# Regrouping tokens by batch and moving transposes to the DMA crossbar in a windowed-attention plus MLP kernel

## The chip, the cores and the metric

The kernel runs on one core of a Trainium2 chip. The metric is the device time of one execution in microseconds (us); smaller is better. Times quoted are medians of all runs of a kernel. Runs marked slow (a lower granted TensorE clock, or over 1.5% above the kernel's fastest run) are left out of ratios. Engine names in the profile: PE is TensorE (PEld is its weight load), DVE is VectorE, ACT is ScalarE, POOL is GpSimd, and SP is SyncE, which here only issues DMAs. A q behind an engine's name means its queue: SPq lines are DMAs that SyncE issues.

## The reference

Eight batches of 576 tokens, eight heads of 64 channels. Causal attention looks back over 64 tokens only; its output `x` (4608 x 512) goes through a layer norm and a two-layer MLP with a residual:

```python
mask   = (rel >= 0) & (rel < 64)                      # sliding window, causal
attn   = softmax(where(mask, q @ k.T / 8, -1e9)) @ v
x      = attn.transpose(0, 2, 1, 3).reshape(8, 576, 512)
xn     = (x - mean(x)) / sqrt(var(x) + 1e-6) * g_ln
out    = x + relu(xn @ w_ch1) @ w_ch2                 # 512 -> 2048 -> 512
```

## The kernel before

The MLP works on groups of four 128-token blocks, 512 tokens at a time, nine groups in all. A group is 32 units of PE work: 16 of layer 1 (four 128x512 matmuls each), then 16 of layer 2. Between the units the kernel slots in the attention of the next batch: score steps (`s_mm`, one or two windows of 64 tokens), the mask on VectorE (`s_mask`), and B steps (`b_step`), which multiply the weights of two windows by V, normalise, take row statistics and leave a centred fp16 block `z`. `zt_step` transposes `z` into the group's `zT`, the moving operand of layer 1. `1/sqrt(var)` of a group (`rstd`, computed partly on GpSimd) scales the output only at the end.

A batch is 4.5 blocks, so in this kernel the groups of four straddle the batches. `vB` is V moved by 64 partitions, made by two copies from SBUF to SBUF (325 and 260 KB) on the GpSimd DMA queue. The parts, with cuts:

```python
def make_vB(b, lo, hi):
    nc.gpsimd.dma_start(out=vB[b][64:128, lo:hi], in_=vA[b][0:64, lo:hi])
    l0, l1 = max(lo - 1, 0), min(hi - 1, 4)
    nc.gpsimd.dma_start(out=vB[b][0:64, l0 + 1:l1 + 1], in_=vA[b][64:128, l0:l1])

def w1_cast(i):
    ...
    nc.gpsimd.tensor_copy(out=w1g[...], in_=t)

def zt_step(kblk, eng=None):
    ...
    ztp = ps_t.tile([128, NKC, 128], FP16, tag="tp", name=f"ztp_{kblk}")
    for kc in range(NKC):
        nc.tensor.transpose(out=ztp[:, kc, :], in_=z[:, 128 * kc:128 * (kc + 1)], identity=ident16)
    ...                                   # copied to zT by ScalarE

# groups 1 to 6: the slots of batch b = g + 1, in units of the group's 32
ss = [2, 7, 12, 17, 22]                   # score steps
sb = [x + 3 for x in ss]                  # B steps, three units after the scores they use
at(13, group_stats, g)
at(0, make_vB, b, 0, 5)
for kblk in range((NW * b) // 2, (NW * (b + 1)) // 2):
    si = sb[((2 * kblk + 1) - NW * b + 1) // 2]
    at(si, b_step, kblk)
    at(max(si + 4, 17 if kblk // 4 > b else 0), zt_step, kblk, "act")
```

The softmax here doesn't subtract the row's maximum and nothing guards it: scores larger than these inputs give would overflow.

## Time and profile before

The first three runs gave 354.6 us (352.95 to 357.05). The lines below are from the page of the profiled execution: the span; busy time, share and instruction count of each engine; then PE's busy share and the granted TensorE clock in 40 equal slices, in tenths; last, the chain of waits that ended last, as shares of the span.

```profile
span 351.7 us, 6792 instructions
...
PE 323.0 (92%) x2778; PEld 159.5 (45%) x2778; DVE 169.0 (48%) x300; ACT 172.9 (49%) x301; POOL 120.5 (34%) x214
...
PE   2662998889999999999999999999999999999995
...
PEclk9999999999999999999999999999999999999998
...
PE 82%; DVE 7%; DMA 4%; SPq 3%; ACT 3%; issue 0%; POOL 0%
```

PE is busy 92% of the span, the clock is full almost everywhere, and 82% of the chain is PE itself. Only the first nine slices (about 80 us) show real holes. The windows view says the same by stage. Its columns are the stretch, its length, then busy time and instruction count of PE, PEld, DVE, ACT and POOL, then the mean granted clock, the DMA share and GB/s. The first stretch is group 1, the second is groups 2 to 5:

```profile
core 0: us, PE busy (x) PEld busy (x) DVE busy (x) ACT busy (x) POOL busy (x), PEclk, DMA share, GB/s
80.30:116.80 36.50, 36.24 (x358) 18.09 (x357) 20.51 (x39) 22.49 (x40) 14.35 (x26) 1.00 0.67 174
116.80:258.60 141.80, 141.74 (x1324) 70.42 (x1322) 75.52 (x139) 84.35 (x146) 50.62 (x88) 1.00 0.60 148
```

Groups 2 to 5 take 141.80 us and PE is busy for 141.74 of them. Whatever takes PE work out of this stretch should shorten the kernel by as much.

| where (timeline and windows of before) | us |
|---|---|
| first layer-1 matmul of group 0 | 35.5 |
| first layer-1 matmul of group 1 | 80.3 |
| first layer-1 matmul of group 2 | 116.8 |
| groups 2, 3, 4, 5 | 35.7, 35.2, 35.7, 35.2 |
| group 6 to the end of the span | 93.1 |

### The profile page before, as it was taken

Reading aid. Unit: us, or ns where it says so; the run is one execution under the profiler, and the core shown is the slowest. Engines: PE = TensorE matmul, PEld = TensorE weight load, DVE = VectorE, ACT = ScalarE, POOL = GpSimd, SP = SyncE. Lnnn points to the kernel's source line nnn. Section 1 sums busy time; section 2 is a strip of 40 time slices with the busy share of each in tenths; the row PEclk is TensorE's granted clock in tenths of the full one; section 3 lists DMA queues with packets and bytes.
Section 4 is the critical chain, followed back from the end, with each engine's and each line's share of the span. In section 5 each row is a group of like instructions: output and inputs, shape, how many; then the busy total and the mean of one; then the engine's idle time right before and its main releaser. Section 6 shows DMA issues by size and latency. Waiting matters only on the chain.

```text
span 351.7 us, 6792 instructions
## 1 busy us (share of the span) xinstructions
PE 323.0 (92%) x2778; PEld 159.5 (45%) x2778; DVE 169.0 (48%) x300; ACT 172.9 (49%) x301; POOL 120.5 (34%) x214
## 2 busy tenths in 40 slices
PE   2662998889999999999999999999999999999995
PEld 1331353454445444544454445444544444444442
DVE  1488066965576167714771667136716671012011
ACT  2331455138735774477447744774477515603600
POOL 4566664863094009400940085008500202001000
PEclk9999999999999999999999999999999999999998
DMA  7999999879934591359235923492310011011011
GB/s 246 248 300 329 177 295 277 264 149 275 254 96 124 172 247 51 100 181 259 55 102 183 234 65 112 150 273 59 114 61 2 2 60 62 0 62 60 0 47 72
DMA packets 73743, 51.16 MB, mean 145 GB/s; under 512 B 47568, under 2 KB 63952, under 8 KB 73712
## 3 DMA queue, kind: packets, MB, share of 16 engines
q1 hardware_dynamic: 72528, 46.41, 49.3%
q0 software_dynamic: 1184, 4.33, 5.3%
q8 instruction: 21, 0.34, 0.4%
q14 instruction: 10, 0.08, 0.1%
HBM read 36.96 MB, written 9.44 MB: 132 GB/s over the span
## 4 chain that ended last, share of the span: by engine, by line
PE 82%; DVE 7%; DMA 4%; SPq 3%; ACT 3%; issue 0%; POOL 0%
DMA w1s_124<-in_moe_w_ch_dram 2%; SPq L115 2%; DMA w1s_442<-in_moe_w_ch_dram 1%; PE ch_1_4109 L328 1%; PE ch_1_3592 L328 1%; PE ch_1_2526 L328 1%; PE ch_1_3076 L328 1%; PE ch_1_2010 L328 1%; PE ch_0_1954 L328 1%; PE ch_0_1406 L328 1%; PE ch_0_3535 L328 1%; PE ch_0_3019 L328 1%; PE ch_0_2470 L328 1%; PE ch_1_1462 L328 1%; PE ch_2_3667 L328 1%; PE ch_2_4177 L328 1%
## 5 line engine op out<-in xcount | busy, mean ns | idle before, releaser
L315 PEld LDWEIGHTS <-w1g 128*128 128x128 f16 x576 | 53.2, 98 | 61.4 <-issue 5.7
L328 PEld LDWEIGHTS <-hrT_4446 128*128 128x128 f16 x64 | 6.3, 98 | 7.5
L328 PEld LDWEIGHTS <-hrT_4255 128*128 128x128 f16 x64 | 6.2, 98 | 7.6
L303 POOL TENSOR_TENSOR rstmp_4532<-rstdg_4531 128x4 f32<-128x4 f32 x2 | 0.4, 198 | 25.4 <-DVE rstdg_4531 L298 25.3
L353 PEld LDWEIGHTS <-hrT_526 128*128 128x128 f16 x64 | 5.8, 98 | 6.7 <-issue 0.8
L338 DVE SCALAR_TENSOR_TENSOR osb_4383<-ch_0_4366,rstdg_4340,xn_3504 128x512 f32<-128x512 f32 x1 | 0.8, 751 | 16.6 <-PE ch_0_4366 L328 16.6
L338 DVE SCALAR_TENSOR_TENSOR osb_4574<-ch_0_4557,rstdg_4531,xn_3935 128x512 f32<-128x512 f32 x1 | 0.8, 751 | 16.2 <-PE ch_0_4557 L328 16.2
L328 PEld LDWEIGHTS <-hrT_3796 128*128 128x128 f16 x64 | 5.8, 98 | 5.8
L328 PEld LDWEIGHTS <-hrT_2216 128*128 128x128 f16 x64 | 5.7, 98 | 5.4
L328 PEld LDWEIGHTS <-hrT_1668 128*128 128x128 f16 x64 | 5.6, 98 | 5.4
L303 POOL TENSOR_TENSOR rstmp_2956<-rstdg_2955 128x4 f32<-128x4 f32 x2 | 0.4, 198 | 22.5 <-DVE rstdg_2955 L298 22.4
L328 PEld LDWEIGHTS <-hrT_2732 128*128 128x128 f16 x64 | 5.6, 98 | 5.4
L303 POOL TENSOR_TENSOR rstmp_4002<-rstdg_4001 128x4 f32<-128x4 f32 x2 | 0.4, 198 | 22.5 <-DVE rstdg_4001 L298 22.4
L303 POOL TENSOR_TENSOR rstmp_1892<-rstdg_1891 128x4 f32<-128x4 f32 x2 | 0.4, 198 | 22.5 <-DVE rstdg_1891 L298 22.4
L328 PEld LDWEIGHTS <-hrT_3280 128*128 128x128 f16 x64 | 5.6, 98 | 5.4
L328 PEld LDWEIGHTS <-hrT_1096 128*128 128x128 f16 x64 | 5.6, 98 | 5.4
L303 POOL TENSOR_TENSOR rstmp_3472<-rstdg_3471 128x4 f32<-128x4 f32 x2 | 0.4, 197 | 21.9 <-DVE rstdg_3471 L298 21.9
L303 POOL TENSOR_TENSOR rstmp_2408<-rstdg_2407 128x4 f32<-128x4 f32 x2 | 0.4, 198 | 21.9 <-DVE rstdg_2407 L298 21.8
L319 ACT ACTIVATE hrT_4446<-hps_0_4447 128x512 f16<-128x512 f32 x1 | 0.6, 597 | 14.1 <-PE hps_0_4447 L315 14.1
L181 DVE COPY qkT_1_493<-tp_0_0_600 128x1024 f16<-128x1024 f16 x1 | 1.2, 1225 | 11.6 <-PE tp_0_0_600 L188 11.6
L188 PE MATMUL tp_0_0_146<-ident_99,qk_0_0_0_142 128*128 128x128 f16 x8 | 1.0, 311 | 5.8 <-POOL qk_0_0_0_142 L96 5.8
L303 POOL TENSOR_TENSOR rstmp_4341<-rstdg_4340 128x4 f32<-128x4 f32 x2 | 0.4, 198 | 17.3 <-DVE rstdg_4340 L298 17.2
(1320 smaller groups left out, 951.2 us busy)
## 6 DMA issues: line engine op xcount, KB each, us to landing
v_0_114<-in_v_dram SPq DMA_DIRECT2D x4, 256.0 KB, 7.5
v_1_478<-in_v_dram SPq DMA_DIRECT2D x4, 256.0 KB, 6.4
v_2_581<-in_v_dram SPq DMA_DIRECT2D x4, 256.0 KB, 4.7
v_3_1297<-in_v_dram SPq DMA_DIRECT2D x4, 256.0 KB, 5.9
v_4_1845<-in_v_dram SPq DMA_DIRECT2D x4, 256.0 KB, 7.3
v_5_2361<-in_v_dram SPq DMA_DIRECT2D x4, 256.0 KB, 6.0
v_6_2909<-in_v_dram SPq DMA_DIRECT2D x4, 256.0 KB, 6.4
v_7_3425<-in_v_dram SPq DMA_DIRECT2D x4, 256.0 KB, 6.7
```

The source lines that it names most:

```text
L115: nc.sync.dma_start(out=v32[b][:, c], in_=v[b, :, 128 * c:128 * c + 128, :].rearrange("h s d -> s h d"),)
L181: nc.vector.tensor_copy(out=out, in_=in_)
L188: nc.tensor.transpose(out=tp[:, i, j, :], in_=src[:, i, j], identity=ident16)
L303: nc.gpsimd.tensor_tensor(out=ab, in0=rs, in1=rs, op=ALU.mult)
L315: nc.tensor.matmul(out=hps, lhsT=w1g[:, kc, 128 * hc:128 * (hc + 1)], rhs=zT[g][:, kc, :], start=(kc == 0), stop=(kc == NKC - 1),)
L319: nc.scalar.activation(out=hrT[:, hc, :], in_=hps, func=AF.Relu, bias=0.0, scale=1.0)
L328: nc.tensor.matmul(out=ch[kb], lhsT=hrT[:, hc, 128 * kb:128 * (kb + 1)], rhs=w2s[:, hc, :], start=(hc == 0), stop=(hc == NHC - 1),)
L338: nc.vector.scalar_tensor_tensor(out=o, in0=ch[kb], scalar=rstd[g][:, kb:kb + 1], in1=x_norm[kblk][:, :, :].rearrange("p h d -> p (h d)"), ...
L353: nc.tensor.matmul(out=ch[kb], lhsT=hrT[:, hc, 128 * kb:128 * (kb + 1)], rhs=w2s[:, hc, :], start=(hc == 0), stop=(hc == NHC - 1),)
```

## The change

Four things at once. (1) A group is now the first 512 tokens of one batch; the eight rests of 64 tokens form group 8. (2) From group 2 on, `z` is transposed by the DMA crossbar, issued on the SP queue, instead of PE and ScalarE. (3) At the start, the W1 casts move from GpSimd to ScalarE and interleave with the B steps of batch 0, most VectorE copies for `vB` of batch 0 (five of eight) become DMAs, the loads of W2 and of batch 1's V move ahead of those of the rests, and the q/k transposes of later work move from group 0 to group 1. (4) Three of four B steps in a group follow a score step directly ("bunched"), to save PE's switching between kinds of matmul. Pools shrink to make room (`xn` 13 to 8 buffers plus 4 for the rests, block pool 4 to 3). The core of the diff, with cuts:

```diff
@@ w1_cast
-        nc.gpsimd.tensor_copy(
+        nc.scalar.copy(
...
@@ zt_step
+        if g >= 2:
+            nc.sync.dma_start_transpose(out=zT[g][:, :, 128 * kb:128 * kb + 128], in_=z)
+            return
...
@@ b_step
-        halves = [divmod(2 * kblk + r, NW) for r in range(2)]
+        halves = [(2 * kb + r, NW - 1) if sfx else (g, 2 * kb + r) for r in range(2)]
...
@@ start
+    make_vB(0, 2, 4)
...
+    for i in range(4):
+        b_step(0, i)
+        if i >= 1:
+            zt_step(0, i - 1)
+        if i < 3:
+            s_mm(0, sets0[i + 2], True)
         w1_cast(i)
         w1_load(i + 4)
+    zt_step(0, 3)
...
@@ group 0
-            at(17, group_stats, 0)
+            at(18, group_stats, 0)
...
@@ groups 1 to 6
-            ss = [2, 7, 12, 17, 22]
-            sb = [x + 3 for x in ss]
+            ss = [1, 6, 11, 16, 21] if g > 1 else [6, 10, 14, 17, 21]
+            for kb in range(4):
+                at(([11, 16, 21, 25] if g > 1 else [14, 17, 21, 25])[kb], b_step, b, kb)
+                at([16, 21, 25, 29][kb], zt_step, b, kb)
+            if b % 2 == 1:
+                at(28, b_step, NGRP - 1, b // 2)
+                at(32, zt_step, NGRP - 1, b // 2)
```

The last block of a group now has its B step at unit 25 and its transpose at unit 29 of 32, just before the group that needs it.

More of the change, by code (lines that the diff above doesn't have):

```diff
@@ L43 @@
     scale = 1.0 / (D ** 0.5)
-    out_f = out.flatten_outer_dims()
     p_const = ctx.enter_context(tc.tile_pool(name="pconst", bufs=1))
@@ L52 @@
     p_pt = ctx.enter_context(tc.tile_pool(name="ppt", bufs=6))
-    p_xn = ctx.enter_context(tc.tile_pool(name="pxn", bufs=13))
-    p_blk = ctx.enter_context(tc.tile_pool(name="pblk", bufs=4))
+    p_xn = ctx.enter_context(tc.tile_pool(name="pxn", bufs=8))
+    p_blk = ctx.enter_context(tc.tile_pool(name="pblk", bufs=3))
     p_grp = ctx.enter_context(tc.tile_pool(name="pgrp", bufs=2))
@@ L136, in make_vB0 @@
         nc.vector.tensor_copy(out=vB[0][64:128, c, :, 0:D], in_=v32[0][0:64, c])
-        nc.vector.tensor_copy(out=vB[0][0:64, c + 1, :, 0:D], in_=v32[0][64:128, c])
+        if c == 0:
+            nc.vector.tensor_copy(out=vB[0][0:64, 1, :, 0:D], in_=v32[0][64:128, 0])
     def make_vB(b, lo, hi):
@@ L239, in v_rhs, with b_step @@
         return vB[b][:, w // 2, h, :]
-    def b_step(kblk):
-        g, kb = divmod(kblk, 4)
-        xn = p_xn.tile([128, H, D], FP32, tag="xn", name=f"xn_{kblk}")
-        x_norm[kblk] = xn
+    def b_step(g, kb):
+        kblk = f"{g}_{kb}"
+        sfx, nb = ("r", 4) if g == NGRP - 1 else ("", None)
+        xn = p_xn.tile([128, H, D], FP32, tag="xn" + sfx, name=f"xn_{kblk}", bufs=nb)
+        x_norm[(g, kb)] = xn
         xps = ps_x.tile([128, H, 128], FP32, tag="xps", name=f"xps_{kblk}")
-        halves = [divmod(2 * kblk + r, NW) for r in range(2)]
+        halves = [(2 * kb + r, NW - 1) if sfx else (g, 2 * kb + r) for r in range(2)]
         for h in range(H):
@@ L263, in b_step @@
         if g not in mvg:
-            mvg[g] = p_grp.tile([128, 4, 2], FP32, tag="mvg", name=f"mvg_{g}", bufs=3)
+            mvg[g] = p_grp.tile([128, 4, 2], FP32, tag="mvg" + sfx, name=f"mvg_{g}", bufs=1 if sfx else 2)
         nc.vector.bn_aggr(out=mvg[g][:, kb, :], in_=stats)
         z = p_blk.tile([128, DM], FP16, tag="z", name=f"z_{kblk}")
-        zsd[kblk] = z
+        zsd[(g, kb)] = z
         nc.vector.scalar_tensor_tensor(
@@ L271, in b_step, with zt_step @@
         )
-    def zt_step(kblk, eng=None):
-        g, kb = divmod(kblk, 4)
-        z = zsd.pop(kblk)
+    def zt_step(g, kb, eng="act"):
+        z = zsd.pop((g, kb))
         if g not in zT:
-            zT[g] = p_grp.tile([128, NKC, 512], FP16, tag="zT", name=f"zT_{g}")
-        ztp = ps_t.tile([128, NKC, 128], FP16, tag="tp", name=f"ztp_{kblk}")
+            sfx = "r" if g == NGRP - 1 else ""
+            zT[g] = p_grp.tile([128, NKC, 512], FP16, tag="zT" + sfx, name=f"zT_{g}", bufs=1 if sfx else 2)
+        if g >= 2:
+            nc.sync.dma_start_transpose(out=zT[g][:, :, 128 * kb:128 * kb + 128], in_=z)
+            return
+        ztp = ps_t.tile([128, NKC, 128], FP16, tag="tp", name=f"ztp_{g}_{kb}")
         for kc in range(NKC):
@@ L323, in l2 @@
         def l2(kb, part):
-            kblk = 4 * g + kb
             if part == 0:
@@ L335, in add_out @@
         def add_out(kb):
-                kblk = 4 * g + kb
-                o = p_blk.tile([128, DM], FP32, tag="osb", name=f"osb_{kblk}")
-                nc.vector.scalar_tensor_tensor(
-                    out=o, in0=ch[kb], scalar=rstd[g][:, kb:kb + 1],
-                    in1=x_norm[kblk][:, :, :].rearrange("p h d -> p (h d)"), op0=ALU.mult, op1=ALU.add,
-                )
-                nc.sync.dma_start(out=out_f[128 * kblk:128 * (kblk + 1), :], in_=o)
-        for hc in range(NHC):
-            units.append(lambda hc=hc: l1(hc))
+            o = p_blk.tile([128, DM], FP32, tag="osb", name=f"osb_{g}_{kb}")
+            nc.vector.scalar_tensor_tensor(
+                out=o, in0=ch[kb], scalar=rstd[g][:, kb:kb + 1],
+                in1=x_norm[(g, kb)][:, :, :].rearrange("p h d -> p (h d)"), op0=ALU.mult, op1=ALU.add,
+            )
+            if g == NGRP - 1:
+                for r in range(2):
+                    nc.sync.dma_start(out=out[2 * kb + r, 512:S, :], in_=o[64 * r:64 * r + 64])
+            else:
+                nc.sync.dma_start(out=out[g, 128 * kb:128 * kb + 128, :], in_=o)
         def l2_hc(i):
@@ L359, in l2_hc @@
                     add_out(kb)
+        for hc in range(NHC):
+            units.append(lambda hc=hc: l1(hc))
         if hc_outer:
@@ L401 @@
         cast_v(0, c, c + 1)
+    make_vB(0, 2, 4)
     sets0 = [[0], [1, 2], [3, 4], [5, 6], [7]]
     s_mm(0, sets0[0], True)
-    make_vB0(0)
     s_mm(0, sets0[1], True)
-    make_vB0(1)
-    for i in range(2, 5):
-        s_mm(0, sets0[i], True)
-        b_step(i - 2)
-        if i < 4:
-            make_vB0(i)
-        if i >= 3:
-            zt_step(i - 3, "act")
-    b_step(3)
-    zt_step(2, "act")
-    zt_step(3, "act")
-    for i in range(4):
+    for c in range(2):
+        make_vB0(c)
+    for i in range(4):
+        b_step(0, i)
[3 more added lines that the diff above has]
+            s_mm(0, sets0[i + 2], True)
         w1_cast(i)
         w1_load(i + 4)
+    zt_step(0, 3)
     load_qk(1, 0)
     load_qk(1, 1)
-    load_qk_rem(0)
-    load_v_rem(0)
+    load_v(1, 0, 4)
     for i in range(4):
         w1_cast(i + 4)
+        w2_load(i)
     cast_qk(1, 0)
     cast_qk(1, 1)
-    cast_qk_rem(0)
-    cast_v_rem(0)
-    load_v(1, 0, 4)
-    load_qk_rem(1)
-    load_v_rem(1)
     alloc_v(1)
@@ L437 @@
     alloc_qkT(1)
-    make_vB(0, 4, 5)
-    cast_v(1, 0, 4)
-    cast_v_rem(1)
-    make_vB(1, 0, 5)
-    for i in range(8):
-        w2_load(i)
-        w2_cast(i)
+    cast_v(1, 0, 4)
+    make_vB(1, 0, 4)
+    for i in range(8):
+        w2_cast(i)
+        if i < 4:
+            w2_load(i + 4)
+    load_qk_rem(0)
+    load_v_rem(0)
+    cast_qk_rem(0)
+    cast_v_rem(0)
+    make_vB(0, 4, 5)
+    load_qk_rem(1)
+    load_v_rem(1)
     SETS = [[0], [1, 2], [3, 4], [5, 6], [7, 8]]
@@ L456 @@
         if g == 0:
-            at(8, t_main, 1, 0, 0, 1)
-            at(9, t_main, 1, 1, 0, 1)
-            at(10, t_main, 1, 0, 1, 1)
-            at(11, t_main, 1, 1, 1, 1)
-            at(12, t_rem, 0)
-            at(12, cast_qk_rem, 1)
-            for i, j in enumerate((12, 13, 14, 15)):
-                at(j, s_mm, 1, SETS[i])
-                at(j, s_mask, 1, SETS[i])
-                if i == 0:
-                    at(14, s_mm, 0, [8])
-                    at(14, s_mask, 0, [8])
-            at(20, t_rem, 1)
@@ L470 @@
-            sb = [17, 18, 19, 20, 21]
-            at(17, group_stats, 0)
-        else:
-            ss = [2, 7, 12, 17, 22]
-            sb = [x + 3 for x in ss]
+            at(9, t_main, 1, 0, 0, 1)
+            at(10, t_main, 1, 1, 0, 1)
+            at(11, t_main, 1, 0, 1, 1)
+            at(12, t_main, 1, 1, 1, 1)
+            for i, j in enumerate((12, 13, 14, 15, 15)):
+                at(j, s_mm, 1, sets0[i])
+                at(j, s_mask, 1, sets0[i])
+            for kb in range(4):
+                at(17 + kb, b_step, 1, kb)
+                at(19 + kb, zt_step, 1, kb)
@@ L475 @@
+            at(18, group_stats, 0)
+            e = 13
+        else:
             at(13, group_stats, g)
-        if g == 1:
-            at(0, s_mm, 1, SETS[4])
-            at(0, s_mask, 1, SETS[4])
-            at(3, b_step, 8)
-            at(7, zt_step, 8, "act")
-        if b < B:
-            if g > 0:
-                for i, ws in enumerate(SETS):
-                    at(ss[i], s_mm, b, ws)
-                    at(ss[i] + 1, s_mask, b, ws)
-                at(0, alloc_vB, b)
-                at(0, make_vB, b, 0, 5)
-            for kblk in range((NW * b) // 2, (NW * (b + 1)) // 2):
-                if kblk == 8 and g == 0:
-                    continue
-                si = sb[((2 * kblk + 1) - NW * b + 1) // 2]
-                at(si, b_step, kblk)
-                dz = 2 if g == 0 else 4
-                at(max(si + dz, 17 if kblk // 4 > b else 0), zt_step, kblk, "act")
+            e = 16
@@ new lines @@
+        if 0 < g and b < B:
+            if g == 1:
+                at(0, t_rem, 0, 0)
+                at(0, cast_qk_rem, 1)
+                at(0, cast_v_rem, 1)
+                at(0, make_vB, 1, 4, 5)
+                at(0, s_mm, 0, [8])
+                at(0, s_mask, 0, [8])
+                at(1, alloc_qkT, 2)
+                at(1, t_main, 2, 0, 0, 0)
+                at(1, t_main, 2, 1, 0, 1)
+                at(2, t_rem, 1, 0)
+                at(2, load_qk_rem, 2)
+                at(2, load_v_rem, 2)
+                at(3, t_main, 2, 0, 1, 0)
+                at(3, t_main, 2, 1, 1, 1)
+                at(4, s_mm, 1, [8])
+                at(4, s_mask, 1, [8])
+                at(7, cast_qk_rem, 2)
+                at(7, cast_v_rem, 2)
+                at(8, b_step, NGRP - 1, 0)
+                at(12, zt_step, NGRP - 1, 0)
+                at(12, t_rem, 2, 0)
+                va = 8
+            else:
+                va = 0
+            at(va, alloc_vB, b)
+            at(va, make_vB, b, 0, 5)
+            ss = [1, 6, 11, 16, 21] if g > 1 else [6, 10, 14, 17, 21]
+            for i, ws in enumerate(SETS):
+                at(ss[i], s_mm, b, ws)
+                at(ss[i] + 1, s_mask, b, ws)
+            for kb in range(4):
+                at(([11, 16, 21, 25] if g > 1 else [14, 17, 21, 25])[kb], b_step, b, kb)
[3 more added lines that the diff above has]
+                at(32, zt_step, NGRP - 1, b // 2)
@@ L495 @@
         if b + 1 < B:
             n = b + 1
-            e = 16 if g > 0 else 12
             at(e - 12, load_qk, n, 0)
             at(e - 11, load_qk, n, 1)
-            at(e - 10, load_qk_rem, n)
+            if g > 0:
+                at(e - 10, load_qk_rem, n)
             at(e - 6, load_v, n, 0, 4)
-            at(e - 6, load_v_rem, n)
+            if g > 0:
+                at(e - 6, load_v_rem, n)
             at(e - 1, cast_qk, n, 0)
             at(e + 1, cast_qk, n, 1)
-            at(e + 3, cast_qk_rem, n)
+            if g > 0:
+                at(e + 3, cast_qk_rem, n)
@@ L506 @@
             at(e + 5, alloc_v, n)
             at(e + 5, cast_v, n, 0, 4)
-            at(e + 6, cast_v_rem, n)
-            at(e + 5, alloc_qkT, n)
-            at(e + 8, t_main, n, 0, 0, 0)
-            at(e + 10, t_main, n, 1, 0, 0)
-            at(e + 12, t_main, n, 0, 1, 0)
-            at(e + 13, t_main, n, 1, 1, 0)
-            at(e + 15, t_rem, n, 0)
+            if g > 0:
+                at(e + 6, cast_v_rem, n)
+            if g > 0:
+                at(e + 5, alloc_qkT, n)
+                at(e + 8, t_main, n, 0, 0, 0)
+                at(e + 8, t_main, n, 1, 0, 0)
+                at(e + 12, t_main, n, 0, 1, 0)
+                at(e + 12, t_main, n, 1, 1, 0)
@@ L515 @@
+            if g > 0:
+                at(e + 16, t_rem, n, 0)
         for i, u in enumerate(units):
```

## The prediction

> **What bounds the kernel now.** TensorE. The page shows PE busy 323.0 of 351.7 us (92%), and the chain of waits lies 82% on PE. The stage windows show two regimes. From 80.3 us (first layer-1 matmul of group 1) to about 348 us PE is busy almost without a wait: groups 1 to 6 take 36.5, 35.7, 35.2, 35.7, 35.2, 33.5 us, groups 7 and 8 (no attention left) 27.7 us each, which is 128 matmuls at 0.216 us. Before 80.3 us PE is idle some 25 us: the first MLP matmul starts at 35.5 us, after VectorE's chain for batch 0 (vB copies 0.4 to 1.15 us each), and the DMA share is about 1.0 until 65 us (17 MB of inputs).
>
> **Costs, from the trace.**
> 1. Transposes: 28 of 36 row blocks leave PE. In the timeline the four transposes of a block cost 0.22 us start to start: 28 x 0.22 = 6.2 us, all in PE-bound groups. ScalarE loses 28 x 0.59 us, off the chain.
> 2. Bunching: a lone score step costs 0.44 us and a lone B step 0.47 us between layer matmuls, of which about 0.2 us is switching. Three of four B steps per group now follow a score step directly: estimate 0.4 us per group, 2.5 us in all.
> 3. New wait: layer 1 of a group waits for the crossbar DMA of z block 3, which the SP queue issues behind the output store of block 2. PE has six layer-2 units (0.87 us each), two q/k transposes and a remainder left, about 6.6 us. VectorE needs 2.8 us for z and 0.75 us for that output, SP 0.4 us, so the DMA has about 2.5 us. The 256 KB stores land in 2.0 us, the SBUF copies in 3.8 to 4.4 us; I estimate 2 to 4 us for 128 KB transposed: 0 to 1.5 us at each of six boundaries, estimate 3 us. The Trainium skill ("VectorE: DVE Perf Modes", The three transpose paths) gives 1309 ns for a crossbar 128x128 against 390 ns on TensorE; no run here shows the former yet.
> 4. Start: five VectorE copies fall away and W1 casts leave GpSimd, so zT of group 0 should be ready near 32 us instead of 35. But W1 loads 4 to 7 wait for ScalarE casts, and ReLU 0 stands behind casts 4 to 7 (about 1 us each), so the third layer-1 unit starts near 37 us (before 38.9). Group 0's outputs still wait for rstd on GpSimd behind the batch-2 casts, which are DMA-bound. Batch 2's q/k transposes (2 us of PE) move from group 0, where PE had slack, into group 1. Group 1 starts at 76 to 82 us and lasts about 38: net gain 2 us, quite uncertain.
>
> **Sum.** 354.6 - 6.2 - 2.5 + 3 - 2 = 347; as the start could gain more, 346 us, 339 to 353. Faster by over 2%: 0.52; within 2%: 0.43; slower: 0.05.
>
> **What would show it.** Groups 2 to 6 each 1 to 1.5 us shorter; PE waits on the transposed tile under 1.5 us; transposes landing in 2 to 4 us; 112 fewer PE matmuls; group 1 starting near 79 us.
>
> **What would make it wrong.** Transposes landing in 5 us or more, or holding the SP queue so that loads come late (slower). A start that is PE-bound rather than DMA-bound (group 1 at 74 us or earlier: 340 us). A PE stall at group 1 because batch-2 casts or rstd come late (350 us or more).

## The result, and the profile after

The changed kernel took 385.77 us (median of 4 runs, 384.04 to 388.71) against 353.77 us for the kernel before (median of 4, 352.17 to 357.05). The ratio is 1.090 (95% interval 1.079 to 1.101): 9% slower, well outside the predicted range. A ratio here is the mean time of one kernel's fast runs over that of the other's fast runs of the same rounds, so it is not quite the ratio of the medians quoted. The kernel before was timed anew with every batch of experiments; its median there was 352.7 to 354.6 us.

The same page lines after the change:

```profile
span 384.4 us, 6620 instructions
...
PE 328.9 (86%) x2666; PEld 159.0 (41%) x2666; DVE 170.1 (44%) x294; ACT 164.8 (43%) x285; POOL 112.7 (29%) x210
...
PE   2776979649869999959996999759998999999994
...
PEclk9999999958989999979998799969999999999999
...
PE 57%; DMA 15%; DVE 14%; issue 7%; POOL 2%; ACT 2%; SPq 2%; DVEq 0%; POOLq 0%; ACTq 0%
```

The 112 PE transposes are gone (2778 to 2666 instructions), as predicted, and yet PE is busy 5.9 us longer. The chain now has 36% on DMA, DVE and "issue" together, where it had 11%. The clock row has a 5, a 6 and several 7s and 8s: PE is slow in places where it was not before.

The windows view of the same two stages (group 1, then groups 2 to 5):

```profile
81.30:130.00 48.70, 43.18 (x392) 21.67 (x392) 26.56 (x44) 22.72 (x42) 20.27 (x36) 0.88 0.68 161
130.00:291.30 161.30, 144.07 (x1252) 69.52 (x1250) 82.05 (x139) 75.14 (x130) 50.09 (x88) 0.94 0.68 144
```

Read the second line against the one before. PE executes 72 instructions fewer, but the stretch is 19.5 us longer: PE idles 161.30 - 144.07 = 17.2 us (before 0.1) and is itself busy 2.3 us longer for less work, at a mean clock of 0.94. The first line (group 1) has PE idle for 5.5 us (before 0.3) and busy 6.9 us longer at a clock of 0.88.

The whole loss by stage, from the group starts in the timeline of the profiled executions:

| stage | before | after | difference |
|---|---|---|---|
| start of the span to group 1 | 80.3 | 81.3 | +1.0 |
| group 1 | 36.5 | 48.7 | +12.2 |
| groups 2 to 5 | 141.8 | 161.3 | +19.5 |
| group 6 to the end | 93.1 | 93.1 | 0.0 |
| sum | 351.7 | 384.4 | +32.7 |

The list of waits names the places. Columns: who waited, for whom, us in total, times, longest.

```profile
PE hps_0_1002 L318 <- DVE osb_0_989 L339: 7.8, 1, 7.8
PE hps_0_3191 L318 <- issue: 6.0, 1, 6.0
...
PE hps_0_2172 L318 <- issue: 4.7, 1, 4.7
PE xps_1_1408 L251 <- DVE pt_3_1318 L233: 3.2, 1, 3.2
PE hps_0_2668 L318 <- DMA zT_2420<-z_3_2602: 2.9, 1, 2.9
...
PE xps_0_1338 L251 <- DMA vB_1220<-vA_869: 1.5, 1, 1.5
...
PE hps_0_3687 L318 <- DMA zT_3439<-z_3_3621: 1.3, 1, 1.3
```

`hps_0_...<-zT` is the first layer-1 matmul of a group. Two of these waits are put down to "issue", meaning that the profile shows no releaser. The timeline shows what landed at that moment. Columns: start, length, engine, instruction; in brackets the idle time before it and its releaser.

```profile
161.29 0.52 POOL L131 MEMSET vB_2178<- 64x520 f16 x1 [4.18 <-PE xps_1_2098 L251]
...
161.76 0.60 POOL L139 DMA_DIRECT2D vB_2178<-vA_2006  x1
...
161.96 1.21 SPq L279 DMA_TRANSPOSE zT_1897<-z_3_2079  x1
...
169.90 1.86 PE L318 MATMUL hps_0_2172<-zT_1897,w1g 128*128 128x512 f16 x4 [4.75 <-issue]
```

The transpose of the last block (`z_3`) of group 3 is issued at 161.96 us. It leaves between the two `vB` copies of the batch after (161.76 and 162.36). These were themselves let loose by a B step, that of the rests (`xps_1_2098`, 160.78 us), which runs just behind the B step of block 3: the memset ahead of them had waited 4.18 us for PE to finish reading the old buffer. The DMA view gives issue to landing (last column, us):

```profile
vB_2178<-vA_2006 POOLq DMA_DIRECT2D x1, 260.0 KB, 6.8
...
zT_1897<-z_2_2004 SPq DMA_TRANSPOSE x1, 2.4
zT_1897<-z_3_2079 SPq DMA_TRANSPOSE x1, 7.8
...
zT_2916<-z_2_3023 SPq DMA_TRANSPOSE x1, 2.4
zT_2916<-z_3_3098 SPq DMA_TRANSPOSE x1, 9.1
...
zT_3912<-z_3_4059 SPq DMA_TRANSPOSE x1, 2.4
```

A transpose that meets nothing lands in 2.4 us; `z_3` of group 3 landed in 7.8 us, at 169.8 us, and layer 1 of group 3 began at 169.90 us. For group 5 the landing was 9.1 us: issued at 244.87, landed at 253.94, first matmul at 254.03. In group 7 no `vB` copies are left to make (batch 7 is the last), and `z_3` landed in 2.4 us again: a control inside the same run. It is not a perfect one: `z_2` of group 7 took 4.0 us, and the store issued 0.4 us before it 3.9 us, with no copy in flight; why stays open.

Before groups 4 and 6 the copies leave earlier and meet `z_2`. Plain output stores (256 KB, 2.0 to 2.3 us alone) that are issued beside the copies are slow as well, so the slowing is not peculiar to transposes. This pair was issued 0.4 us apart, right behind the copies before group 4:

```profile
out_dram<-osb_1_2545 SPq DMA_DIRECT2D x1, 256.0 KB, 6.2
...
zT_2420<-z_2_2527 SPq DMA_TRANSPOSE x1, 7.8
```

The same pair before group 6 took 5.9 and 6.0 us.

The loss in group 1 begins with the 7.8 us wait at its start, shown by the timeline:

```profile
76.92 1.04 POOL L94 CAST qk_1_2_1_730<-qk_1_2_1_547 128x1024 f16<-128x1024 f32 x1 [0.53 <-DMA qk_1_2_1_547<-in_k_dram]
...
80.28 0.20 POOL L309 TENSOR_TENSOR rstdg_855<-rstdg_855,rstmp_856 128x4 f32<-128x4 f32 x1
...
80.51 0.75 DVE L339 SCALAR_TENSOR_TENSOR osb_0_989<-ch_0_774,rstdg_855,xn_0_241 128x512 f32<-128x512 f32 x1 [9.18 <-POOL rstdg_855 L309]
...
81.32 1.89 PE L318 MATMUL hps_0_1002<-zT_880,w1g 128*128 128x512 f16 x4 [7.80 <-DVE osb_0_989 L339]
```

Layer 1 needs a PSUM buffer that `osb_0` frees. `osb_0` needs `rstd`, whose GpSimd part stands in its queue behind the casts of batch 2, which wait for their loads until 76.92 us. The next matmuls run cold: four take 1.89 us, where the same four took 1.04 us before.

### The profile page after: what moved, and what is told of

Same layout as the page of the kernel before. It is cut to its first block, busy times and chain, and to the rows that moved or that the text cites. A ratio compares the mean times of both kernels' runs of the same rounds, so it can differ in the third digit from the quotient of the medians.

```text
span 384.4 us, 6620 instructions
## 1 busy us (share of the span) xinstructions
PE 328.9 (86%) x2666; PEld 159.0 (41%) x2666; DVE 170.1 (44%) x294; ACT 164.8 (43%) x285; POOL 112.7 (29%) x210
## 4 chain that ended last, share of the span: by engine, by line
PE 57%; DMA 15%; DVE 14%; issue 7%; POOL 2%; ACT 2%; SPq 2%; DVEq 0%; POOLq 0%; ACTq 0%
DMA w2s_467<-in_moe_w_ch_dram 2%; DMA qk_1_2_1_547<-in_k_dram 2%; DMA qk_1_0_1_112<-in_k_dram 2%; DMA vB_1220<-vA_869 2%; DMA w2s_497<-in_moe_w_ch_dram 2%; DMA w1s_436<-in_moe_w_ch_dram 1%; DMA zT_2420<-z_3_2602 1%; PE ch_1_1453 L330 1%; PE ch_0_3886 L330 1%; PE ch_0_2890 L330 1%; PE ch_2_1529 L330 1%; DVE pt_3_1318 L233 1%; PE ch_3_2092 L330 1%; PE ch_3_4485 L330 1%; PE ch_3_3111 L330 1%
## 5 line engine op out<-in xcount | busy, mean ns | idle before, releaser
L318 PEld LDWEIGHTS <-w1g 128*128 128x128 f16 x576 | 55.6, 102 | 95.1 <-issue 32.1
L330 PEld LDWEIGHTS <-hrT_1001 128*128 128x128 f16 x64 | 6.3, 104 | 7.8 <-issue 2.2
L330 PEld LDWEIGHTS <-hrT_4120 128*128 128x128 f16 x64 | 6.3, 98 | 7.5
L330 PEld LDWEIGHTS <-hrT_4311 128*128 128x128 f16 x64 | 6.2, 97 | 7.6
L330 PEld LDWEIGHTS <-hrT_3686 128*128 128x128 f16 x64 | 5.9, 98 | 6.8
L330 PEld LDWEIGHTS <-hrT_3190 128*128 128x128 f16 x64 | 5.9, 98 | 6.5
L330 PEld LDWEIGHTS <-hrT_2667 128*128 128x128 f16 x64 | 5.9, 98 | 6.5
L330 PEld LDWEIGHTS <-hrT_1648 128*128 128x128 f16 x64 | 5.9, 98 | 6.5
L330 PEld LDWEIGHTS <-hrT_2171 128*128 128x128 f16 x64 | 5.9, 98 | 6.5
L318 PE MATMUL hps_0_1002<-zT_880,w1g 128*128 128x512 f16 x4 | 1.9, 628 | 7.8 <-DVE osb_0_989 L339 7.8
L356 PEld LDWEIGHTS <-hrT_522 128*128 128x128 f16 x64 | 5.8, 98 | 6.3 <-issue 0.4
L306 POOL TENSOR_TENSOR rstmp_4397<-rstdg_4396 128x4 f32<-128x4 f32 x2 | 0.4, 198 | 26.0 <-DVE rstdg_4396 L301 25.9
L306 POOL TENSOR_TENSOR rstmp_2861<-rstdg_2860 128x4 f32<-128x4 f32 x2 | 0.4, 198 | 25.6 <-DVE rstdg_2860 L301 25.5
L306 POOL TENSOR_TENSOR rstmp_3384<-rstdg_3383 128x4 f32<-128x4 f32 x2 | 0.4, 198 | 25.4 <-DVE rstdg_3383 L301 25.3
L306 POOL TENSOR_TENSOR rstmp_2365<-rstdg_2364 128x4 f32<-128x4 f32 x2 | 0.4, 198 | 25.2 <-DVE rstdg_2364 L301 25.1
L94 POOL CAST qk_0_1_0_469<-qk_0_1_0_444 128x1024 f16<-128x1024 f32 x1 | 1.0, 1040 | 20.7 <-DMA qk_0_1_0_444<-in_q_dram 20.7
L318 PE MATMUL hps_0_3191<-zT_2916,w1g 128*128 128x512 f16 x4 | 1.9, 620 | 6.0 <-issue 6.0
L306 POOL TENSOR_TENSOR rstmp_3861<-rstdg_3860 128x4 f32<-128x4 f32 x2 | 0.4, 198 | 21.1 <-DVE rstdg_3860 L301 21.0
```

The source lines that it names most:

```text
L94: nc.gpsimd.tensor_copy(out=dst[:, :].rearrange("p a j e d -> p a e j d"), in_=t[:, :].rearrange("p (a e) j d -> p a e j d", e=2),)
L306: nc.gpsimd.tensor_tensor(out=ab, in0=rs, in1=rs, op=ALU.mult)
L318: nc.tensor.matmul(out=hps, lhsT=w1g[:, kc, 128 * hc:128 * (hc + 1)], rhs=zT[g][:, kc, :], start=(kc == 0), stop=(kc == NKC - 1),)
L330: nc.tensor.matmul(out=ch[kb], lhsT=hrT[:, hc, 128 * kb:128 * (kb + 1)], rhs=w2s[:, hc, :], start=(hc == 0), stop=(hc == NHC - 1),)
L356: nc.tensor.matmul(out=ch[kb], lhsT=hrT[:, hc, 128 * kb:128 * (kb + 1)], rhs=w2s[:, hc, :], start=(hc == 0), stop=(hc == NHC - 1),)
```

## The experiments

Theories for groups 2 to 5:

- **Collision.** The transpose of block 3 is slow because the `vB` copies are in flight with it, and it is on the critical path because regrouping made it the last thing before its group. Then either moving the `vB` copies behind it or keeping a lead should bring back nearly all 19 us.
- **Rival: the crossbar itself.** Transposes on the SP queue are slow or hold up loads whatever else is in flight. Then the old grouping with the crossbar must also be slow.
- **Rival: the schedule.** Regrouping and bunching cost PE time by themselves. Then the changed kernel with PE transposes must also be slow in groups 2 to 5.

Theories for the start and group 1: the late `rstd` wait and the slow clock after it; the W1 casts on ScalarE, which delay the loads; or only PE work moved from group 0 to group 1.

All kernels gave correct results. Diffs are against the kernel named.

### 1. The changed kernel with its transposes back on PE

```diff
-        if g >= 2:
+        if g >= 99:
             nc.sync.dma_start_transpose(...)
```

> The changed kernel with all z transposes back on TensorE (112 transposes), nothing else undone. Theory A (the loss in groups 2 to 5 is PE waiting at the group's start for crossbar transposes that are held up by the vB copies, 15.5 us of waits at the five starts of groups 3 to 7 plus about 5 us of cold clock): 385.8 - 20 + 5 = about 368 to 373 us, groups 3 to 7 start without a wait of over 0.5 us. Rival B (regrouping and bunching themselves cost it, for instance by late z or late scores): 383 us or more, waits at the group starts stay.

Measured: 367.68 us, before 354.58, ratio 1.037 (1.032 to 1.042). Groups 2 to 5 took 141.0 us with PE busy 140.98 us for 1323 instructions (before 141.8 us for 1324). So the schedule does not cost PE time there; regrouping and bunching together gain 0.8 us over four groups, 0.2 us each (one profile of each kernel). The rival of the schedule falls for groups 2 to 5. Group 2 starts at 126.4 us instead of 116.8: the loss of the start is here without any crossbar.

### 2. The changed kernel with the vB copies behind the transposes

```diff
     def make_vB(b, lo, hi):
-        nc.gpsimd.dma_start(out=vB[b][64:128, lo:hi], in_=vA[b][0:64, lo:hi])
+        q = nc.sync if b >= 2 else nc.gpsimd
+        q.dma_start(out=vB[b][64:128, lo:hi], in_=vA[b][0:64, lo:hi])
...
```

The SP queue issues in order, so the copies now follow the last transpose.

> The changed kernel with the vB copies of batches 2 to 7 issued from the SP queue, behind the last transpose of the group, instead of from GpSimd's queue. Theory A1 (a transpose is slow only while the vB copies move): transposes land in 2.4 to 3 us, starts of groups 3 to 7 wait under 1 us each, 362 to 370 us. Rival A2 (the transposes of a group's end are slow for another reason, such as output stores or the q/k loads after them): some still land in 5 us or more, 380 us or more.

Measured: 363.67 us, before 354.58, ratio 1.026 (1.021 to 1.030), against 1.090 for the changed kernel. The windows (group 1, groups 2 to 5):

```profile
81.00:126.30 45.30, 42.74 (x392) 21.54 (x392) 25.82 (x44) 22.72 (x42) 19.10 (x32) 0.88 0.65 159
126.30:268.30 142.00, 137.69 (x1251) 68.11 (x1248) 82.20 (x139) 75.14 (x130) 45.84 (x80) 1.00 0.71 165
```

and the DMA view (28 transposes together, median landing last):

```profile
vB<-vA SPq DMA_DIRECT2D x6, 260.0 KB, 4.4
...
zT<-z SPq DMA_TRANSPOSE x28, 2.5
```

Groups 2 to 5 fall from 161.3 to 142.0 us, with the same PE instructions (1252 and 1251). The 19.3 us divide into 12.9 us less idle time (17.2 to 4.3) and 6.4 us less busy time (144.07 to 137.69), as the clock is back at 1.00. The transposes land in 2.5 us (median; the longest in 4.4). This is the collision, shown by taking it away. What stays is about 2.5 us of waits for `zT` in this kernel: with a landing of 2.5 us the transpose still has hardly any lead. In this grouping the crossbar gains nothing even so: with PE transposes (experiment 1) groups 2 to 5 took 141.0 us.

### 3. The statistics of group 0 earlier

```diff
-            at(18, group_stats, 0)
+            at(8, group_stats, 0)
```

> The changed kernel with the rstd of group 0 computed ten slots earlier, so before the casts of batch 2 on GpSimd. Theory C (the 7.8 us wait at the start of group 1 is rstd queued behind casts that wait for their loads; with it goes the cold clock of the first layer matmuls): the wait goes, group 1 starts at 73 to 76 us instead of 81.3, 375 to 380 us. Rival D (group 1 needs the batch 2 casts anyway, for q/k transposes in its second slot): the wait only moves into the first slots of group 1, 384 us or more.

Measured: 383.75 us, before 354.58, ratio 1.072 (1.063 to 1.081), but two of its four runs, the profiled one among them, are marked slow, so its times are not compared, and its timeline is told only for where the wait went. There the wait at the start of group 1 is 0.27 us instead of 7.8, and group 1 starts at 76.5 us. It then lasts 54.2 us: the fourth output had no buffer (the block pool has three) until a store behind the V loads on the SP queue had left, 5.87 us of waiting. The wait moved more than it went. Inconclusive as to the time.

### 4. The kernel before with the crossbar alone

```diff
@@ before, zt_step
+        if g >= 2:
+            nc.sync.dma_start_transpose(out=zT[g][:, :, 128 * kb:128 * kb + 128], in_=z)
+            return
```

> The kernel before with only the crossbar transposes from group 2 added; its groups straddle batches. Theory E (crossbar transposes cost nothing where the block is ready well ahead; the regrouping took that lead away): no PE wait over 0.5 us at group starts, 28 x 0.22 us off PE, 347 to 350 us, even if some transposes land in 5 to 9 us. Rival F (crossbar transposes disturb the queue or the other copies wherever they stand): 354 us or more.

Measured: 348.04 us, before 354.58, ratio 0.981 (0.977 to 0.985): faster than both kernels. Windows (group 1, groups 2 to 5):

```profile
81.00:116.10 35.10, 35.10 (x338) 16.88 (x338) 21.05 (x39) 19.98 (x35) 15.22 (x29) 1.00 1.00 198
116.10:254.00 137.90, 137.90 (x1251) 66.16 (x1250) 77.61 (x139) 74.88 (x128) 50.75 (x88) 1.00 0.76 169
```

Groups 2 to 5 take 137.9 us, 3.9 us less than before, for 73 PE instructions fewer, and PE has no idle time at all. (Its interval lies below 1, but whether the gain reaches 2% is unclear.) The rival of the crossbar itself falls: its gain is about 1.0 us a group, as predicted. And yet at least one transpose of each batch collides here too. This is the one issued at 143.05 us, beside `vB` copies issued at 142.80 and 143.40:

```profile
zT<-z SPq DMA_TRANSPOSE x1, 8.6
```

Nobody waits for it. By the order of issue it carries block 16, which in the old grouping is the first block of group 4, while group 3 is about to start. Block 16 landed at 151.64 and group 4 began at 185.0. Block 15, the last that group 3 needs, was issued at 138.54, met no copies, landed 2.4 us later, and was used at 150.8. The tightest case is block 11, the last that group 2 needs. It was issued at 108.29 between the two copies of its batch:

```profile
zT<-z SPq DMA_TRANSPOSE x1, 7.2
```

It landed at 115.54, and group 2 began at 116.07 without a wait: a lead of 7.8 us from issue to use was just enough. So the collision alone costs nothing; collision without lead costs 19 us.

| groups 2 to 5 | `vB` copies issued beside a transpose | `vB` copies behind the transposes |
|---|---|---|
| last block just before its group (new grouping) | changed kernel: 161.3 us | experiment 2: 142.0 us |
| last block with a lead (old grouping) | experiment 4: 137.9 us; experiment 9, bunched: 137.2 us | experiment 13, bunched: 137.1 us |

### 5. Experiment 4 with the new start

```diff
@@ experiment 4
-        nc.gpsimd.tensor_copy(          # w1_cast
+        nc.scalar.copy(
...                                      # and the new order of batch 0, as in the change
```

> e4_before_xbar (348.0 us) with the changed kernel's start for batch 0: W1 cast on ScalarE, vB of blocks 2 and 3 by DMA, loop reordered. Theory G (the first 80 us are bound by loads, so an earlier first layer-1 matmul is given back before group 1): layer 1 starts at 31 to 32 us instead of 34.5, group 1 starts at 79 to 83 us as before, 346 to 351 us. Rival H (the start is on the chain, the changed kernel only loses it by its load order later): group 1 starts 3 to 4 us earlier, 344 to 345 us.

Measured: 354.24 us, before 352.79, ratio 1.006 (0.999 to 1.013), against 0.981 for experiment 4. Layer 1 of group 0 starts 3.5 us earlier (31.0 against 34.5), but group 1 starts 4.8 us later (85.8 against 81.0). The new start loses, without the regrouping. The SP queue's W1 loads (start, time until the last has left, count) are shown with experiment 10.

### 6. Experiment 2 with matmuls that keep PE warm

```diff
@@ experiment 2, after the slots of group 0
+        if g == 0:
+            keep = ps_x.tile([128, H, 128], FP32, tag="xps", name="keep_warm")
+            for _ in range(24):
+                nc.tensor.matmul(out=keep[:, 0:4, :], lhsT=ident16, rhs=w2s[:, 0, :], start=True, stop=True)
```

> e2_vb_on_sp (363.7 us) with 24 useless 128x512 matmuls (24 x 0.216 = 5.2 us) at the end of group 0, in the 5.4 us in which PE waits for rstd and the outputs of group 0. Theory I (half of what this wait costs is the cold clock after it, the first layer matmuls of group 1 at 0.43 us apart instead of 0.216): group 1 starts at the same 81 us, its first units take 0.87 us instead of 1.7, 359 to 361 us though work was added. Rival J (group 1 is held by its operands, not by the clock): 363 us or more.

Measured: 358.5 us, before 352.79, ratio 1.015 (1.011 to 1.020), against 1.026 (1.021 to 1.030) for experiment 2. Adding 24 matmuls whose result nobody reads made the kernel faster. Group 1 in this kernel:

```profile
82.70:124.30 41.60, 38.48 (x394) 19.90 (x394) 25.40 (x44) 22.63 (x42) 18.73 (x32) 1.00 0.72 174
```

Against experiment 2 (42.74 us of PE work at a clock of 0.88) group 1 has 38.48 us at 1.00, for the same instructions within two. The wait at the start of group 1 costs twice, by itself and by 4.3 us of slow clock after it. Against before (36.24 us, 358 instructions) 2.2 us remain, for 36 PE instructions more: work that the change moved here from group 0.

### 7. Experiment 2 with early statistics, outputs of group 0 in place

This one writes the outputs of group 0 over `x`.

```diff
@@ experiment 2
-            o = p_blk.tile([128, DM], FP32, tag="osb", name=f"osb_{g}_{kb}")
+            if g == 0:
+                o = x_norm[(0, kb)][:, :, :].rearrange("p h d -> p (h d)")
+            else:
+                o = p_blk.tile([128, DM], FP32, tag="osb", name=f"osb_{g}_{kb}")
...
-            at(18, group_stats, 0)
+            at(8, group_stats, 0)
```

> e2_vb_on_sp with rstd of group 0 computed before the batch-2 casts and the outputs of group 0 written into their x tile, so that no output buffer has to come free (in e3_early_stats the fourth output waited 5.9 us for a store that stood behind the loads of V on the SP queue). Theory K (the start of group 1 is held only by that chain of rstd and output buffer): group 1 starts at 75 to 77 us and ends about 4 us earlier than in e2, 358 to 360 us. Rival L (regrouping put work of batches 1 and 2 that waits for late loads into the first slots of group 1): the wait moves to the second or third slot of group 1, group 2 starts at 125 to 127 us as in e2, 362 to 365 us.

Measured: 360.61 us, before 352.79, ratio 1.020 (1.014 to 1.026); experiment 2 had 1.026 (1.021 to 1.030), so the gain is not clear. Group 1 starts at 76.5 us instead of 81.0, but lasts 48.0 us instead of 45.3, and two later waits have grown: 2.30 us for a cast of a q/k rest on GpSimd, and 4.10 us for `vB`. The wait for `rstd` was one of several late arrivals of the same loads; removing it exposed the next.

### 8. Experiment 4 bunched tightly

```diff
@@ experiment 4
-            sb = [x + 3 for x in ss]
+            sb = [7, 12, 17, 22, 25]
```

> e4_before_xbar (348.0 us) with each B step placed directly behind the next score step in groups 1 to 6, as in the changed kernel. Predicted was 0.4 us per group; e1 against the kernel before gives only about 0.2 us per group (35.5, 34.8, 35.8, 34.8, 33.5 against 35.7, 35.2, 35.7, 35.2, 33.5 us). With 0.2: 346.5 to 347.5 us; with 0.4: 345 to 346 us; if z now comes too late for its group: PE waits at a group start and 349 us or more.

Measured: 362.06 us, before 352.79, ratio 1.026 (1.022 to 1.031), where experiment 4 had 0.981. Groups 2 to 5:

```profile
116.10:267.10 151.00, 142.83 (x1251) 70.39 (x1250) 79.73 (x139) 75.50 (x128) 50.23 (x88) 0.95 0.70 155
```

151.0 us against 137.9. The last B step of a batch stands three units after its scores, and VectorE is now in the middle of the preceding B step's chain when the mask is due. VectorE in group 2:

```profile
141.63 1.99 DVE L268 SCALAR_TENSOR_TENSOR z<-xn,mvg,gB 128x512 f16<-128x512 f32 x1
...
144.21 0.67 DVE L234 TENSOR_TENSOR pt<-pt,mask 128x1024 f16<-128x1024 f16 x1
```

and PE, where the B step waits and the matmuls that follow are slow:

```profile
144.94 0.22 PE L251 MATMUL xps<-vA,pt 128*64 128x65 f16 x1 [2.11 <-DVE pt L234]
...
147.05 3.15 PE L331 MATMUL ch<-w2s,hrT 128*128 128x512 f16 x8
```

The mask (L234) runs behind an output and `z` (L268), which took 1.99 us here instead of its usual 0.75; GpSimd's cast of V (141.17 to 143.08) ran beside it. PE idles 2.11 us, and two us later eight 128x512 matmuls take 3.15 us, where eight take 1.89 at the full clock. The windows view shows the clock (third column from the right): full in the stretch that holds the wait, half in the next.

```profile
142.76:146.17 3.41, 1.30 (x21) 0.74 (x21) 2.83 (x5) 0.25 (x1) 3.05 (x7) 1.00 0.46 127
146.17:149.59 3.42, 3.42 (x15) 1.76 (x14) 2.41 (x5) 1.01 (x1) 0.00 (x0) 0.50 0.98 178
```
So bunching is a trade with VectorE's order. The idle time of groups 2 to 5 is 8.2 us, and PE's work is 4.9 us longer for the same 1251 instructions.

### 9. Experiment 4 bunched with room

```diff
-            ss = [2, 7, 12, 17, 22]
-            sb = [x + 3 for x in ss]
+            ss = [1, 6, 11, 16, 21]
+            sb = [6, 11, 16, 21, 26]
```

> e4_before_xbar (348.0 us) bunched as e8_xbar_bunched was, but with the changed kernel's spacing: score steps at slots 1, 6, 11, 16, 21 and the last B step at 26, five units behind instead of three. In e8 (362.1 us) that last B step waited 2.0 us for the mask on VectorE in each group, with a cold clock after it. Theory M (only the room was missing): no such wait, groups 1 to 6 each 0.2 us shorter than in e4, 346 to 348 us. Rival N (VectorE cannot hold a bunched order in any spacing): waits stay, 352 us or more.

Measured: 347.59 us, before 352.7, ratio 0.985 (0.980 to 0.989): no different from experiment 4 (0.977 to 0.985). Groups 2 to 5 take 137.2 us against 137.9, again under 0.2 us a group. Five units between scores and B step take the 2 us wait away; what bunching gains is too small to be seen in the time.

### 10. Experiment 5 with the W1 casts back on GpSimd

```diff
-        nc.scalar.copy(
+        nc.gpsimd.tensor_copy(
```

> e5_xbar_new_start (354.2 us) with the W1 casts back on GpSimd, all else of the new start kept. In e5 the last W1 load left the SP queue at 29.6 us instead of 23.5, and every later load 4 to 6 us later. Theory O (the wait of W1 loads 4 to 7 for the ScalarE casts in batch 0's loop shifts all later loads): last W1 load at 23 to 24 us, group 1 starts at 79 to 82 us instead of 85.8, 347 to 350 us. Rival P (the vB copies by DMA or the reordered loop do it): 353 us or more.

Measured: 349.74 us, before 352.7, ratio 0.991 (0.986 to 0.995, one slow run of six left out), clear of experiment 5 (0.999 to 1.013). The eight W1 loads on the SP queue, first experiment 5, where the casts are on ScalarE:

```profile
11.72 17.91 SPq L151 DMA_DIRECT2D w1s<-in_moe_w_ch_dram  x8
```

then this one:

```profile
11.92 14.26 SPq L151 DMA_DIRECT2D w1s<-in_moe_w_ch_dram  x8
```

The last load leaves at 26.2 instead of 29.6 us (23.5 in experiment 4). W1 loads 4 to 7 wait for buffers that the casts free; on ScalarE the casts stand between exponentials and transposes of batch 0, and every load behind them on the queue is late. Group 1 starts at 83.0 us instead of 85.8. It is still 2.0 us later than in experiment 4, so the rest of the new start does not gain either; why its loads still leave 2.7 us later was not taken apart.

### 11. Experiment 2 with the W1 casts on GpSimd

```diff
-        nc.scalar.copy(
+        nc.gpsimd.tensor_copy(
```

> e2_vb_on_sp (363.7 us) with the W1 casts back on GpSimd. Theory O for the changed kernel itself: all loads about 5 us earlier, rstd of group 0 near 75 us, group 1 starts at 75 to 78 us instead of 81, 356 to 360 us. Rival Q (the rest of the loss in groups 0 and 1 comes from regrouping alone): group 1 at 80 us or later, 362 us or more.

Measured: 360.26 us, before 352.7, ratio 1.021 (1.018 to 1.025); experiment 2 had 1.021 to 1.030. The direction is that of experiment 10, but the intervals overlap. Group 2 starts at 122.5 us instead of 126.3, and a wait of 4.88 us for `osb` stays at the start of group 1.

### 12. All mends together

Experiment 7 plus experiment 11: `vB` copies behind the transposes, early statistics, outputs of group 0 in place, W1 casts on GpSimd.

```diff
@@ experiment 7
-        nc.scalar.copy(
+        nc.gpsimd.tensor_copy(
```

> The changed kernel with the three single repairs together: vB copies behind the transposes (e2), rstd and outputs of group 0 freed early (e7), W1 casts back on GpSimd (e11). If these were all that the regrouped order lost: 347 to 350 us, level with e4_before_xbar. If regrouping in itself costs time in groups 0 and 1 (q/k transposes of batch 2 and remainders of batches 0 and 1 moved from group 0, where PE waits for loads, into group 1): group 1 lasts 43 us or more against 36.5, 354 to 358 us.

Measured: 355.47 us, before 352.86, ratio 1.006 (1.001 to 1.012), with one slow run of six left out of the ratio. Group 1 starts at 73.3 us, the earliest of all kernels, and then:

```profile
73.30:118.60 45.30, 39.85 (x393) 20.08 (x394) 25.32 (x44) 22.73 (x42) 18.73 (x34) 0.96 0.70 169
```

It lasts 45.3 us, with 39.85 us of PE work for 393 instructions (before 36.24 for 358) and 5.4 us of idle time, most of it one wait for `vB` of batch 2, whose copies stand in the SP queue:

```profile
97.45 0.19 PE L252 MATMUL xps<-vB,pt 128*64 128x65 f16 x1 [3.61 <-DMA vB<-vA]
```

Group 2 starts at 118.6 us, against 116.1 in experiment 4, and groups 2 to 5 take 141.7 us against 137.9. With the known faults mended the change brings the kernel back to about where it was before, and no further. The earlier start is paid back in group 1, and the new grouping still pays in groups 2 to 5, in part for its short lead (waits of 0.88 and 1.45 us for `zT`).

### 13. Experiment 9 with the vB copies on SP

```diff
@@ experiment 9
-        nc.gpsimd.dma_start(...)        # both copies of make_vB
+        eng = nc.sync if b >= 2 else nc.gpsimd
+        eng.dma_start(...)
```

> e9_xbar_bunched_roomy (347.6 us) with the vB copies of batches 2 to 7 on the SP queue, so that no transpose runs beside them. If lead alone is enough (as e4 says), nothing is gained but the 0.7 us wait at group 2: 346 to 348 us, transposes near 2.4 us. If the slow transposes cost something even with the lead: 344 to 346 us. If the copies now come late behind loads: 349 us or more.

Measured: 345.89 us, before 352.86, ratio 0.980 (0.973 to 0.987), one slow run of six left out of the ratio. The 0.7 us wait at group 2 is gone. Its transposes land in 2.8 us (median), but two take 6.0 and 6.6 us. Both were issued (87.67 and 124.48 us) after the copies had landed (84.93 and 120.39), while loads of q and k were in flight: the copies are not the only DMAs beside which a transpose is slow. It has the lowest median of all, but its interval covers that of experiment 4 and most of that of experiment 9, so it is not shown to beat them. It is about 2% faster than the kernel before.

## Why the prediction was wrong, point by point

**What bounds the kernel: right.** PE-bound in groups 1 to 6; experiment 4 turned 73 PE instructions fewer into 3.9 us.

**Step 1, transposes: right in size.** It named 0.22 us a block, 6.2 us in all. Experiment 4 has about 1.0 us a group and 6.5 us in the medians. In the changed kernel the 112 matmuls are gone as predicted.

**Step 2, bunching: the term was too large.** Predicted 0.4 us a group; experiments 1 and 9 show about 0.2 us, from one profile each and in experiment 1 together with regrouping. That it comes from PE's switching, as the step says, is not shown.

**Step 3, "New wait": this is the step that failed.** It estimated "0 to 1.5 us at each of six boundaries, estimate 3 us". Its lead was right: it gave the DMA "about 2.5 us", and in the trace 3.2 us passed between the issue of `z_3` of group 3 and PE running dry (161.96 to 169.90 - 4.75 = 165.15). Its landing time was wrong: "2 to 4 us" holds for a transpose that meets nothing (2.4 us), but the one that counts landed in 7.8, 4.8 and 9.1 us before groups 3, 4 and 5 (the 4.8 us after a late issue, behind a transpose that took 7.8). I took landing times from the profile of before and did not ask what else would be issued at that moment. Before groups 3 and 5 the B step of the rests, which follows that of block 3, releases the buffer for the next `vB` copies; before groups 4 and 6 the copies follow GpSimd's casts of V. In this order of work the two meet before each of these groups. The Trainium skill ("DMA: Bandwidth & Descriptors", Issuing engines are not separate DMA queues) says that DMAs issued by different engines run on the same 16 DMA engines and interleave; the 7.8 us against 2.4 us agree. Waits of 15 us at the starts of groups 3 to 6 are the direct cost; the second part, which the prediction did not have at all, is the clock. In groups 2 to 5 the measured price is 19.3 us (experiment 2).

**Step 4, "net gain 2 us": failed too.** Two of its numbers were right: layer 1 of group 0 starts at 31.3 us ("near 32"), and group 1 starts at 81.3 us ("76 to 82"). The second is luck: PE had run dry at 73.5 us, and a 7.8 us wait that the step had not priced brought the start back into the range. Wrong was that group 1 "lasts about 38": it lasted 48.7. The step itself named the risk (`rstd` behind the batch-2 casts) and gave it no cost. The extra 12.2 us of group 1 are, by the windows view, 5.3 us of idle time and 6.9 us of PE work; of the latter experiment 6 shows 4.3 us to be slow clock and about 2.2 us moved work. Among the waits is one of 3.2 us for a mask on VectorE, `pt_3`:

```profile
108.70 3.57 DVE L233 TENSOR_TENSOR pt_3_1318<-pt_3_1318,mask 128x1024 f16<-128x1024 f16 x1
```

The same operation takes 0.67 us in experiment 8's lines. Beside it GpSimd cast q, k and V of batch 3, one after the other. The Trainium skill ("SBUF — State Buffer", SBUF: two separate sides) states that VectorE and GpSimd share a port pair as an exclusive lock: of an operation of VectorE with two SBUF inputs and one of GpSimd that reads SBUF, the one that starts later is blocked. The trace fits that: in the changed kernel all ten masks of this shape that overlap a GpSimd cast take 1.09 to 3.57 us, and the 17 others 0.68 to 0.69 us. That is a regularity of the trace; no run here changed GpSimd's work alone. W1 on ScalarE costs by delaying loads (experiments 5 and 10). The 7.8 us wait before group 1 lies in group 0's stretch; the earlier start (31.3 instead of 35.5 us) paid for 4.2 us of it. No run took back the new order of loads alone, so what it does to group 1 stays open.

**What the sum left out: the clock.** The Trainium skill ("TensorE: Matmul & The Clock Gate", What's actually happening) gives a half-rate state after about 3.4 us of idle PE. It should have been a term of every wait in the prediction. Here it agrees in kind: after the waits of 5 to 8 us four matmuls take 1.86 to 1.89 us instead of 1.04. But waits of 2.95 us (before group 4) and of 2.11 us (experiment 8) were followed by slow matmuls as well.

**The odds.** Both dangers that did it were written down ("Transposes landing in 5 us or more", "A PE stall at group 1"), and "slower" still got only 0.05. Since the transposes were a kind of DMA that no trace of the kernel had shown, the chance was set too low.

**What stays open.** How the DMAs in flight share the engines. Stores beside the copies are slowed like the transposes (6.2 and 7.8 us), so it is not the crossbar alone; but no run varied the size of the copies, and experiment 2 changes their queue and their order at once.

## What to carry to other kernels

When work moves from a full engine to a DMA, price the landing at the moment of its issue, with what else is in flight then, and check how long before its use it is issued: a transpose of 7.2 us cost nothing where it was issued 7.8 us ahead of its use, and such transposes cost 19 us over four groups where PE ran dry 3 us after the issue. Price an idle stretch of PE as the wait plus the slow matmuls after it. And try each part of a bundle alone: here one of four parts carried nearly all the gain (experiment 4, about 2%). With the other three the bundle was 9% slower, and with its known faults mended (experiment 12) it gained nothing.

## What the Trainium skill lacked or had wrong

- "Advanced Engine Details and Errata", X-Bar Transpose (TRN2): "TRN2 transpose DMAs are as fast as regular DMAs". No run here tests it at equal size: alone a transpose of 128 KB took 2.4 us and a store of 256 KB 2.0 us or a little more, and beside SBUF copies both were slow (7.8 and 6.2 us). What no page gives is a transpose's time beside other DMAs: issued within 0.4 us of the copies it took 7.2 to 9.1 us in the changed kernel and in experiment 4, and the copies 5.2 to 8.4 us.
- "VectorE: DVE Perf Modes", The three transpose paths: 1309 ns for a crossbar transpose of 128x128 and 390 ns on TensorE stand there without saying what is counted. For a 128x512 block the trace has 2.4 us from issue to landing (and 1.2 us of the SP queue), against 0.22 us of PE for four transposes in a filled PE queue; the ratio from the table is no guide to a schedule.
- "TensorE: Matmul & The Clock Gate", What's actually happening: about 3.4 us of idle before the half rate. In experiment 8 an idle PE of 2.11 us was followed by a granted clock of 0.50 from 146.17 to 149.59 us, and eight matmuls took 3.15 us instead of 1.89. In the kernel before, an idle PE of 1.92 us (69.78 to 71.70) was followed by no drop, so a rule for short waits does not come out of these runs.
- "SBUF — State Buffer", SBUF: two separate sides: the lock is described, but with no time for a two-input VectorE operation beside a run of GpSimd casts. Here one took 3.57 us instead of 0.67.
